# Second half of a weights' product from split factors in three passes

## The chip, the cores and the metric

One core of one Trainium2 chip runs the whole program. The metric is the device time of one execution in microseconds (us). The kernel before took 1076.94, 1076.49 and 1073.06 us in three runs; the median is 1076.49 us.

The engines are named as the profile names them: PE (TensorE, matrix products), PEld (its weight loads), ACT (ScalarE), DVE (VectorE), POOL (GpSimd) and SP (SyncE, which issues most DMAs here). Each works through its own queue strictly in the order in which the program wrote it.

## The reference

An attention over chunks of 32 queries with 56 neighbouring keys and 8 memory keys feeds two gated layers:

```python
attn_out = _attn_ref(**attn_kwargs)             # 4 x 8 heads x 768 x 64
x = attn_out.transpose(0, 2, 1, 3).reshape(B * S, H * D)     # 3072 x 512
# layer 1, d_ff = 1024
a, b = x @ w1, x @ w2
h = a * b @ w3
x = h @ w_out
# layer 2, d_ff = 1536
return ((x @ w_a) * (x @ w_b)) @ w_out2
```

Nothing nonlinear stands between `w3` and `w_out` of layer 1, so the kernel first forms their product W = w3 @ w_out (1024 x 512) and applies it once. The change is in the making of W.

## The kernel before, in words

**Formats.** Most products are made from two parts of each factor: a high part that is the value rounded to the type `float32r`, and a low part that is the value minus the high part. Three matrix passes (high by high, high by low, low by high: `PASSES`) then stand for the float32 product. The product W alone is made in plain `float32`.

**Weights.** The weights arrive as 64-bit words and have to be turned into float32 first. A block goes through a pipeline: `w_load` (DMA, issued on SP, into a raw buffer), `w_scale` (two ACT instructions, lines 372 and 373), `w_sum` (two DVE instructions, lines 377 and 378). Blocks 0 to 7 (`w3a`) hold a row block of `w3` for the first half and the row block of `w_out`; blocks 8 to 11 (`w3b`) hold two row blocks of `w3` each for the second half, so block 8 serves k = 0 and 1 of the second half, block 9 serves k = 2 and 3, and so on; blocks 12 to 27 (`w12`) are the weights w1 and w2, which are split into parts by ACT (line 414) and DVE (line 408). `w_tick` moves every block in the pipeline one step on and issues the next load when a raw buffer is free. In the text, "scale 9" and "sum 9" are these steps of block 9.

**The product W.** Two halves, each 8 steps of k by 4 output tiles m, that is 32 calls of `mm` on 128x128 by 128x512; line 570. Four PSUM banks hold the four tiles; `w_evict` (lines 563 on ACT, 564 on DVE) empties them at the end of a half. After each second call the program drops other work into the engines' queues, by a counter g = 0 to 15: a `w_tick` at listed g, and an `attn_slot`.

**Attention in slots.** Attention goes unit by unit (192 queries, all heads). `attn_slot` takes the next slot of a list made beforehand; slot 0 is at g = 9 of the first half, slot 6 at its g = 15, slots 7 to 22 are g = 0 to 15 of the second half. The stages of a unit: `a_keys` (DVE copy, line 154), `a_scores` (PE, tile sc), `a_max` (DVE, lines 192 and 193), `a_exp` (ACT, line 201, in four parts of 4 exponentials, two parts to a slot), `a_norm` in two parts (DVE lines 216 and 217, then POOL line 218), `a_trans` (PE transposes, tile pt, line 229), `a_pt` (ACT, line 235), `a_pv` (PE, tile xp), `a_x` (ACT line 99, DVE line 102). The slots that matter here: unit 0's scores and all its exponentials in slot 0, its norms in slot 2, its transposes in slot 6 with the scores of unit 1 behind them; unit 1's exponentials in slots 7 and 8, its norms in 8 and 9, its transposes in 12; unit 2's scores in 13, maxima and first exponentials in 14, norms in 15 and 16, transposes in 19, `a_pt` in 20, `a_pv` in 21, `a_x` in 22.

**After W.** The loop over six token blocks follows (`ab_step`: psA and psB, line 619; then psY). The first one needs unit 2's `a_x`. Between its products further `w_tick`s and attention slots are issued. The rest of the program (second layer in a seven-product scheme, lines 812 to 871) follows in the same manner.

**Buffers.** Converted blocks 0 to 11 lie two by two in buffers of the tag "w12" (8 of them in all, which rotate and later hold the split w1 and w2); raw blocks 0 to 11 lie in 4 rotating buffers "raw2".

Of the kernel before, what the change touches and what calls it, by code (L numbers as in the profile page):

```python
# [7 lines left out]
F32 = mybir.dt.float32  # L8
F32R = mybir.dt.float32r
U32 = mybir.dt.uint32  # L10
AF = mybir.ActivationFunctionType
ALU = mybir.AluOpType

P = 128
# [23 lines left out]
CH = 512  # L38
# [7 lines left out]
def tile_attention_moe(  # L46
# [16 lines left out]
    nc = tc.nc  # L63
# [4 lines left out]
    wpool = ctx.enter_context(tc.tile_pool(name="wpool", bufs=8))  # L68
# [4 lines left out]
    p0 = p0stack.enter_context(tc.tile_pool(name="p0", bufs=3))  # L73
# [15 lines left out]
    def mm(o, l, r, first, last):  # L89
        nc.tensor.matmul(o, lhsT=l, rhs=r, start=first, stop=last)  # L90
# [7 lines left out]
    def split_hi(hi, src):  # L98
        nc.scalar.activation(hi, src, AF.Copy)  # L99
# [10 lines left out]
    def a_k(u):  # L110
        if u >= NA:
            return
        k = ks[u] = att.tile([P, NE, 4 * KW], F32, tag="kraw", bufs=1, name="kraw")
        src = kt[2 * NE * u, D : 2 * D].rearrange("d h k -> d (h k)")
        row, x = src.ap
        step = 2 * 2 * D * row[0]
        src = bass.AP(src.tensor, src.offset, [[row[0], P], [step, NE], x])
        nc.sync.dma_start(out=k, in_=src)

    def a_q(u):  # L120
        if u >= NA:
            return
        q = qs[u] = att.tile([P, NE, 4 * GQ], F32, tag="q", bufs=1, name="q")
        src = qt[2 * NE * u : 2 * NE * u + 2 * NE]
        nc.sync.dma_start(
            out=q, in_=src.rearrange("(e r) d h q -> (r d) e (h q)", r=2)
        )
# [18 lines left out]
    def a_keys(u):  # L146
        if u >= NA:
            return
        k = ks.pop(u).rearrange("p e (h k) -> p (e h) k", h=4)
        p, a, e = k.ap  # L150
        win = bass.AP(
            k.tensor, k.offset + NMEM * e[0], [p, a, [CHUNK * e[0], NC], [e[0], KEYS - NMEM]]
        )
        nc.vector.tensor_copy(kw[:, :, :, NMEM:], win)  # L154
        if new_batch(u):
            nc.vector.tensor_copy(
                kw[:, :, :, 0:NMEM], k[:, :, None, 0:NMEM].to_broadcast([P, NH, NC, NMEM])
            )
# [153 lines left out]
    def attn_slot(n=1):  # L312
        for _ in range(n):
            s = acount[0]
            if s >= NEED[-1]:
                return
            acount[0] += 1
            for stage_of, u in todo.get(s, []):
                stage_of(u)
# [18 lines left out]
    def w_tile(i, tag, shape):  # L338
        x = int(tag == "raw2")
        if i < NW0 and tag == "dec":  # L340

            x = int(turn[tag][1] * BUFS[tag][0] < turn[tag][0] * BUFS[tag][1])
        n = BUFS[tag][x]
        if live[tag][x] == n:
            return None, x
        turn[tag][x] += 1
        live[tag][x] += 1
        return (stage, p0)[x].tile(shape, U32, tag=tag, bufs=n, name=tag), x
# [26 lines left out]
    def w_bits(a, r):  # L375
        l, h = r[:, :, 0], r[:, :, 1]
        nc.vector.tensor_scalar(a, h, 3, None, ALU.logical_shift_left)
        nc.vector.tensor_tensor(a, a, l, ALU.add)  # L378
# [5 lines left out]
    def pieces_of(i, *tiles):  # L384
        return [[t[:, c0:c1] for t in tiles] for c0, c1 in pieces(i)]

    def w_sum(i, r):
        kind, f = plan[i][:2]
        if kind == "w12":
            a, ax = w_tile(i, "dec", [P, CH])  # L390
            w_bits(a, r)
            return a.bitcast(F32), ax
        if f % 2 == 0:
            pairs["f"] = wpool.tile([P, 2, 2 * CH], U32, tag="w12", name="w3_f")
        a = pairs["f"][:, f % 2, :]
        for a1, r1 in pieces_of(i, a, r):
            w_bits(a1, r1)
        if kind == "w3a":
            w3k[f], wo_f[f] = a[:, :CH], a[:, CH:]
        else:  # L400
            w3k[8 + 2 * f], w3k[9 + 2 * f] = a[:, :CH], a[:, CH:]
        return None, None

    def w_turn():

        if len(pipe[2]):
            i, a, ax, (d, f, w, hi, lo) = pipe[2].pop(0)
            nc.vector.tensor_tensor(lo, a, hi.bitcast(F32), ALU.subtract)  # L408
            live["dec"][ax] -= 1
            d[f] = w  # L410
        if pipe[1]:
            i, a, ax = pipe[1].pop(0)
            t = w_place(*plan[i][:3])
            nc.scalar.activation(t[3], a, AF.Copy)
            pipe[2].append((i, a, ax, t))
        if len(pipe[0]):
            i, r, tag = pipe[0].pop(0)
            a, ax = w_sum(i, r)
            live[tag][int(tag == "raw2")] -= 1
            if ax is not None:  # L420
                pipe[1].append((i, a, ax))

    def w_next():
        if wraw:
            i, r, tag = wraw.pop(0)
            for (r1,) in pieces_of(i, r):
                w_scale(r1)
            pipe[0].append((i, r, tag))
        while w_load():
            pass  # L430

    def w_tick():
        w_turn()
        w_next()
# [3 lines left out]
    wsm, w3k, wo_f, w12s = {}, {}, {}, {}  # L438
    pairs = {}
# [4 lines left out]
    def w_place(kind, m, c):  # L444

        if c == 0:
            pairs[kind] = wpool.tile([P, 2, 2 * CH], F32R, tag="w12", name="w12")
        w = pairs[kind][:, :, CH * c : CH * (c + 1)]
        v = pairs[kind].rearrange("p l (k j f) -> p l k j f", k=KD, j=2)
        return (w12s if c else {}), m, v, w[:, 0, :], w[:, 1, :]  # L450
# [92 lines left out]
    PASSES = ((0, 0), (0, 1), (1, 0))  # L543
# [17 lines left out]
    def w_evict(half, m):  # L561
        w = wsm[4 * half + m] = w_new(wpool, "wo")
        nc.scalar.activation(w[:, 0, :], banks[m], AF.Copy)
        nc.vector.tensor_tensor(w[:, 1, :], banks[m], w[:, 0, :].bitcast(F32), ALU.subtract)

    for half in range(2):
        banks = [psd.tile([P, 512], F32, tag="d", name="wps") for _ in range(4)]
        for k in range(8):
            for m in range(4):
                mm(  # L570
                    banks[m],
                    w3k[8 * half + k].bitcast(F32)[:, P * m : P * m + P],
                    wo_f[k].bitcast(F32),
                    k == 0,
                    k == 7,
                )
                if k == 7 and m > 0:
                    w_evict(half, m - 1)
                if m % 2 == 0:
                    continue  # L580
                g = 2 * k + m // 2
                if half == 0:
                    if g >= 9:
                        attn_slot()
                    if g in (0, 2, 4, 6, 8, 9):
                        w_tick()
                    if g == 0:
                        a_k(0)
                        a_q(0)
                    if g == 7:  # L590
                        a_keys(0)
                        a_k(1)
                    if g == 9:
                        bound[0] = len(wsrc)
                    if g == 13:
                        w_turn()
                else:
                    attn_slot()
                    if g == 0:
                        w_next()  # L600
                    if g in (1, 4, 5, 6, 9, 10, 11, 12):
                        w_tick()
        w_evict(half, 3)
    del pairs["f"]
    wo_f.clear()
    w3k.clear()
    p0stack.close()

# [421 lines left out]
```

## Time and profile before

| | before |
|---|---|
| median of three runs | 1076.49 us (1073.06 to 1076.94) |
| profiled execution: span from its first to its last instruction | 1073.7 us |
| PE busy | 1058.5 us, 99% |
| ACT busy | 444.0 us, 41% |
| DVE busy | 452.7 us, 42% |
| POOL busy | 233.1 us, 22% |
| PE busy with the product W (tile wps) | 59.2 us |

The profile has one time for the profiled execution, its span; no time around it is recorded, so the span is taken as that execution's own time. It lies 2.8 us under the median and 0.6 us above the lowest of the three runs. Shares are averages over the whole span. In the first 130 us weights arrive, W is made and attention runs between, and DVE and ACT are far busier there than these averages; from about 127 us on PE works without a gap.

A plain float32 call of `mm` shows as two matmul records, a pass on `float32r` operands as one.

### The profile page before, as it was taken

The page shows a single profiled execution, that of the slowest core. Times are in us where ns is not written, and L with a number is a line of the kernel's source. Part 1 is how long each engine was busy: PE and PEld are TensorE (multiplying, and loading weights), DVE is VectorE, ACT ScalarE, POOL GpSimd, SP SyncE. Part 2 cuts the span into 40 slices and gives each one's busy share as a digit, 9 for nine tenths or more (in the row PEclk, how much of TensorE's full clock was granted, in tenths as well). Part 3 has the DMA queues.
Part 4 walks back from the last instruction along what each step waited for, and adds up shares of the span by engine and source line. Part 5 has one row for each costly group of instructions (what it writes and reads, how often), then busy time and mean ns, then how long its engine had stood idle before and what let it go on. Part 6 is the DMA issues. An engine that isn't in the chain of part 4 may idle for free.

```text
span 1073.7 us, 18442 instructions
## 1 busy us (share of the span) xinstructions
PE 1058.5 (99%) x7442; PEld 846.3 (79%) x7442; DVE 452.7 (42%) x751; ACT 444.0 (41%) x1153; POOL 233.1 (22%) x228
## 2 busy tenths in 40 slices
PE   9989899999999999999999999999999999999998
PEld 3457788888888888888888888888888888888886
DVE  5567734435435434346653434432322253223310
ACT  6867654436636543535443343332222232222210
POOL 0102312202303302212033222112233202222210
PEclk9999999999999999999999999999999999999999
DMA  9964474454454462364555554524344433433311
GB/s 365 312 194 158 124 198 146 130 166 146 150 184 118 140 188 86 108 230 143 196 198 206 204 185 157 186 92 154 137 151 173 160 113 139 172 139 138 137 40 39
DMA packets 62342, 172.02 MB, mean 160 GB/s; under 512 B 6321, under 2 KB 21553, under 8 KB 56369
## 3 DMA queue, kind: packets, MB, share of 16 engines
q1 hardware_dynamic: 51680, 104.75, 30.2%
q0 software_dynamic: 10368, 66.06, 17.0%
q8 instruction: 58, 0.95, 0.4%
q14 instruction: 28, 0.22, 0.1%
q10 hardware_dynamic: 208, 0.04, 0.0%
HBM read 137.27 MB, written 33.55 MB: 159 GB/s over the span
## 4 chain that ended last, share of the span: by engine, by line
PE 87%; DVE 1%; ACT 0%; issue 0%; ACTq 0%
PE ps L816 31%; PE ops L90 18%; PE psY L90 12%; PE psB L90 11%; PE psA L90 11%; PE xp L90 2%; PE sc L90 1%; PE pt L229 1%; DVE x L102 0%; DVE tmp L670 0%; ACT x L99 0%; DVE kw L154 0%; DVE w L408 0%; DVE tmp L833 0%; ACT tmp L892 0%
## 5 line engine op out<-in xcount | busy, mean ns | idle before, releaser
L816 PE MATMUL ps<-x,w 128*128 128x512 f32 x1512 | 348.7, 389 | 0.3 <-ACT tmp L828 0.3
L816 PEld LDWEIGHTS ps<-x,w 128*128 128x128 f32 x1512 | 283.6, 188 | 60.1 <-ACT tmp L828 1.4
L833 DVE TENSOR_TENSOR tmp<-ps,tmp 128x512 f32<-128x512 f32 x108 | 74.6, 690 | 261.1 <-PE ps L816 231.0
L90 PE MATMUL psA<-xt,w 128*128 128x512 f32 x576 | 141.7, 394 | 3.0 <-DVE w L408 3.0
L90 PE MATMUL psB<-xt,w 128*128 128x512 f32 x576 | 140.0, 392 | 0.0
L90 PE MATMUL psY<-g,wo 128*128 128x512 f32 x576 | 135.7, 392 | 0.0
L635 POOL TENSOR_TENSOR g<-gv,g 128x512 fp32r<-128x512 f32 x48 | 65.1, 1356 | 305.4 <-ACT g L634 305.4
L828 ACT ACTIVATE tmp<-ps 128x512 f32<-128x512 f32 x108 | 64.6, 599 | 157.8 <-PE ps L816 151.3
L90 PEld LDWEIGHTS psA<-xt,w 128*128 128x128 f32 x576 | 107.3, 188 | 27.9 <-DVE w L408 3.8
L90 PEld LDWEIGHTS psB<-xt,w 128*128 128x128 f32 x576 | 107.2, 188 | 22.5
L90 PEld LDWEIGHTS psY<-g,wo 128*128 128x128 f32 x576 | 107.0, 188 | 22.4
L700 POOL DMA_DIRECT2D w<-wc x72 | 39.7, 553 | 373.6 <-PE ps L816 373.5
L90 PE MATMUL ops<-wo,g 128*128 128x512 f32 x504 | 118.6, 389 | 0.0
L90 PEld LDWEIGHTS ops<-wo,g 128*128 128x128 f32 x504 | 94.6, 188 | 19.6
L839 ACT ACTIVATE g<-tmp 128x512 fp32r<-128x512 f32 x66 | 40.7, 633 | 139.8 <-DVE tmp L838 139.8
L840 POOL TENSOR_TENSOR g<-tmp,g 128x512 fp32r<-128x512 f32 x66 | 84.1, 1294 | 20.4 <-ACT g L839 19.4
L201 ACT ACTIVATE t<-sc,mx 96x64 f32<-96x64 f32 x256 | 75.5, 317 | 25.3 <-DVE mx L193 25.2
L90 PE MATMUL ops<-fo,g 128*128 128x512 f32 x288 | 68.2, 389 | 0.0
L90 PEld LDWEIGHTS ops<-fo,g 128*128 128x128 f32 x288 | 54.1, 188 | 11.2
L90 PE MATMUL wps<-w_f 128*128 128x512 f32 x128 | 59.2, 614 | 0.5 <-DVE w_f L378 0.4
L218 POOL TENSOR_TENSOR t<-t,sm 96x512 f32<-96x512 f32 x32 | 36.8, 1150 | 101.9 <-DVE sm L217 95.4
L372 ACT ACTIVATE raw<-raw 128x512 f32<-128x512 f32 (+1 forms) x66 | 49.3, 748 | 11.4 <-DMA raw<-in_w3a 8.0
(65 smaller groups left out, 878.1 us busy)
## 6 DMA issues: line engine op xcount, KB each, us to landing
w<-wc POOLq DMA_DIRECT2D x36, 1024.0 KB, 6.9
w<-wc POOLq DMA_DIRECT2D x36, 768.0 KB, 5.0
wc<-co SPq DMA_DIRECT2D x84, 256.0 KB
raw<-in_wab SPq DMA_DIRECT2D x24, 512.0 KB
v<-in_vw SPq DMA_DIRECT2D x64, 168.0 KB
kraw<-in_kt SPq DMA_DIRECT2D x16, 512.0 KB
raw<-in_w SPq DMA_DIRECT2D x16, 512.0 KB
raw<-in_w3a SPq DMA_DIRECT2D x6, 1024.0 KB
```

The costliest lines, as they stand in the source:

```text
L90: nc.tensor.matmul(o, lhsT=l, rhs=r, start=first, stop=last)
L201: nc.scalar.activation(t[:, a, r, :], sc[:, r, a, :], AF.Exp, bias=mx[:, r, a : a + 1], scale=SCALE, accum_out=sm[:, a, r : r + 1],)
L218: nc.gpsimd.tensor_tensor(t, t, sm[:, :, :, None].to_broadcast([GQ, 4, 2, KEYS]), ALU.mult)
L229: nc.tensor.transpose(pt[:, a // 4, a % 4, :], t[:, a].rearrange("p r k -> p (r k)"), id_sb)
L372: nc.scalar.activation(h, h, AF.Prelu, scale=2.0**-112, alpha=2.0**32)
L635: nc.gpsimd.tensor_tensor(g2[:, 1, :], gv, g2[:, 0, :].bitcast(F32), ALU.subtract)
L700: nc.gpsimd.dma_start(out=t[:, c0:c1].bitcast(F32), in_=src[:, c0:c1])
L816: nc.tensor.matmul(ps, lhsT=w[:, i, a, k, :], rhs=xs[i][:, b, k, :], start=first and n == 0, stop=n == 5, skip_group_check=not first,)
L828: nc.scalar.activation(z, ps, AF.Copy)
L833: nc.vector.tensor_tensor(z, ps, y, ALU.add)
L839: nc.scalar.activation(g2[:, 0, :], z, AF.Copy)
L840: nc.gpsimd.tensor_tensor(g2[:, 1, :], z, g2[:, 0, :].bitcast(F32), ALU.subtract)
```

## The change

The second half's 32 calls become 32 times three passes on split parts. The split parts of `w3` (name w3h, hi and lo in one tile) are made from each of blocks 8 to 11 by `w_cut`: one ACT copy and one POOL subtraction of 128x1024 each, into the rotating raw2 buffers. It is called at g = 9 to 15 of the first half and, ahead of the attention slot, at every g of the second; it does nothing as long as no summed block waits. The parts of `w_out` (wo_h) are made in the first half, after each k, by `wo_cut`: one ACT copy and one POOL subtraction of 128x512, into buffers of the tag w12. Loads, scales, sums, evictions and the first half's matmuls are as before.

```diff
         if kind == "w3a":
             w3k[f], wo_f[f] = a[:, :CH], a[:, CH:]
         else:
-            w3k[8 + 2 * f], w3k[9 + 2 * f] = a[:, :CH], a[:, CH:]
+            cut.append((f, a.bitcast(F32)))
         return None, None
+
+    w3h, woh, cut = {}, {}, []
+
+    def w_cut():
+        if cut:
+            f, a = cut.pop(0)
+            x = p0.tile([P, 2, 2 * CH], F32R, tag="raw2", bufs=4, name="w3h")
+            split_hi(x[:, 0], a)
+            nc.gpsimd.tensor_tensor(x[:, 1], a, x[:, 0].bitcast(F32), ALU.subtract)
+            for k in range(2):
+                w3h[2 * f + k] = x[:, :, CH * k : CH * k + CH]
+
+    def wo_cut(k):
+        if k % 2 == 0:
+            pairs["h"] = wpool.tile([P, 2, 2, CH], F32R, tag="w12", name="wo_h")
+        x = pairs["h"][:, k % 2]
+        a = wo_f[k].bitcast(F32)
+        split_hi(x[:, 0], a)
+        nc.gpsimd.tensor_tensor(x[:, 1], a, x[:, 0].bitcast(F32), ALU.subtract)
+        woh[k] = x
...
+                if half == 0:
+                    mm(
+                        banks[m],
+                        w3k[k].bitcast(F32)[:, P * m : P * m + P],
+                        wo_f[k].bitcast(F32),
+                        k == 0,
+                        k == 7,
+                    )
+                else:
+                    for i, (a, b) in enumerate(PASSES):
+                        mm(
+                            banks[m],
+                            w3h[k][:, a, P * m : P * m + P],
+                            woh[k][:, b],
+                            k == 0 and i == 0,
+                            k == 7 and i == 2,
+                        )
...
                     if g == 13:
                         w_turn()
+                    if g >= 9:
+                        w_cut()
+                    if m == 3:
+                        wo_cut(k)
                 else:
+                    w_cut()
                     attn_slot()
```

In the queues this stands as follows. In the first half `wo_cut(4)` is written at g = 9, behind unit 0's 16 exponentials and scale 8 on ACT, and ahead of unit 0's norms (g = 11) on POOL. At g = 13 come sum 8, `w_cut` of block 8 and `wo_cut(6)`; at g = 15 `wo_cut(7)`. In the second half `w_cut` of block 9 stands at g = 2 (sum 9 is at g = 1), of block 10 at g = 5 and of block 11 at g = 6.

## Rows read from the trace of the kernel before

**Rows 1.** The page: the chain that ended last, share of the span by engine.

```profile
PE 87%; DVE 1%; ACT 0%; issue 0%; ACTq 0%
```

**Rows 2.** The chain in order of time, its start and a later stretch: start, length, what.

```profile
125.29 0.77 DVE kw L154
...
126.71 1.21 PE psA L90 x4
...
165.52 2.72 PE psA L90 x12
```

**Rows 3.** By stretch: busy us of PE, PEld, DVE, ACT, POOL; clock, DMA share.

```profile
74.00:77.00 3.00, 0.32 (x13) 0.18 (x14) 1.58 (x3) 2.16 (x4) 0.00 (x0) 1.00 0.82 225
77.00:84.00 7.00, 6.96 (x102) 4.14 (x99) 3.22 (x6) 3.03 (x7) 0.00 (x0) 0.52 0.79 236
```

**Rows 4.** Timeline of PE: start, length, line, operation; idle before and its releaser.

```profile
27.27 10.57 PE L90 MATMUL wps<-w_f 128*128 128x512 f32 x24
37.68 0.82 PE L229 MATMUL pt<-id_sb,t 96*128 96x96 f32 x8
40.59 1.18 PE L90 MATMUL sc<-kw,q 64*32 64x64 f32 x96 [2.08 <-DMA q<-in_qt]
41.70 5.42 PE L90 MATMUL wps<-w_f 128*128 128x512 f32 x12
47.05 1.60 PE L90 MATMUL xp<-p,v 64*64 64x32 f32 x96
...
56.59 1.19 PE L90 MATMUL sc<-kw,q 64*32 64x64 f32 x96
...
70.51 3.62 PE L90 MATMUL wps<-w_f 128*128 128x512 f32 x8
76.82 2.50 PE L90 MATMUL xp<-p,v 64*64 64x32 f32 x96 [2.69 <-ACT p L235]
79.25 3.78 PE L90 MATMUL wps<-w_f 128*128 128x512 f32 x4
82.50 4.04 PE L90 MATMUL psA<-xt,w 128*128 128x512 f32 x12
```

**Rows 5.** Timeline of ACT, the product W's stretch.

```profile
27.41 1.14 ACT L372 ACTIVATE raw<-raw 128x1024 f32<-128x1024 f32 x1 [2.64 <-DMA raw<-in_w3a]
...
34.11 1.17 ACT L372 ACTIVATE raw<-raw 128x1024 f32<-128x1024 f32 x1
...
36.17 2.31 ACT L563 ACTIVATE wo<-wps 128x512 fp32r<-128x512 f32 x4
...
43.33 0.31 ACT L201 ACTIVATE t<-sc,mx 96x64 f32<-96x64 f32 x1 [3.98 <-DVE mx L193]
...
52.08 0.84 ACT L99 ACTIVATE xt<-xp 128x768 fp32r<-128x768 f32 x1
...
61.13 0.31 ACT L201 ACTIVATE t<-sc,mx 96x64 f32<-96x64 f32 x1 [3.09 <-DVE mx L193]
```

**Rows 6.** Timeline of DVE, the same stretch.

```profile
34.91 1.69 DVE L154 COPY kw<-kraw 128x1344 f32<-128x1344 f32 x1 [0.22 <-DMA kraw<-in_kt]
...
37.34 1.23 DVE L378 CUSTOM_DVE_ANT_0 w_f<-raw,w_f 128x2048 uint16<-128x2048 uint16 x1
...
48.11 1.22 DVE L378 CUSTOM_DVE_ANT_0 w_f<-raw,w_f 128x2048 uint16<-128x2048 uint16 x1
...
53.83 0.85 DVE L154 COPY kw<-kraw 128x1344 f32<-128x1344 f32 x1
...
66.69 1.42 DVE L378 CUSTOM_DVE_ANT_0 dec<-raw,dec 128x1024 uint16<-128x1024 uint16 x1
```

**Rows 7.** Timeline of POOL, the same stretch.

```profile
34.84 1.04 POOL L218 TENSOR_TENSOR t<-t,sm 96x512 f32<-96x512 f32 x1 [1.30 <-DVE sm L217]
...
66.51 1.05 POOL L218 TENSOR_TENSOR t<-t,sm 96x512 f32<-96x512 f32 x1 [1.20 <-DVE sm L217]
```

**Rows 8.** POOL subtractions of one tile: min/median/max ns, first and last start.

```profile
L635 POOL TENSOR_TENSOR g<-gv,g x48: 1279/1295/1786, 94.2 to 508.9; 128x512 fp32r<-128x512 f32 x48
```

More of the change, by code (lines that the diff above doesn't have):

```diff
@@ L569, in tile_attention_moe @@
             for m in range(4):
[L570 to L576, printed above, removed]
+                if half == 0:
[15 more added lines that the diff above has]
+                        )
                 if k == 7 and m > 0:
@@ L603, in tile_attention_moe @@
         w_evict(half, 3)
-    del pairs["f"]
+    del pairs["f"], pairs["h"]
     wo_f.clear()
+    woh.clear()
+    w3h.clear()
     w3k.clear()
```

## The prediction

> **What bounds the kernel now.** I read the chain of waits first: 87% of the span is PE [rows 1], and traced back from the end the chain is PE with hardly a break until 126.7 us, where it leaves PE for DVE (key copy, then w1/w2) [rows 2]. From there on nothing in this change matters; what counts is when PE gets to 126.7. The stretches tell where PE is not the bound before that: it is busy 0.32 of 3 us in 74 to 77 and then works 7 us at a granted clock of 0.52, that is 1.2 GHz nearly throughout [rows 3]. PE's own timeline gives the half in question: the second half begins at 41.70, scores of unit 2 stand at 56.59, PE then waits 2.69 us at 76.82 for ACT's `a_pt` of unit 2, and psA begins at 82.50 [rows 4]. That wait is the end of a chain of maxima, exponentials, norms, sums 13 and 14, loads and scales, not of matmuls: PE was through with its calls at 74.1 (70.51 + 3.62). So the second half is set by the attention's chain on ACT and DVE, with PE 2.7 us ahead of it.
>
> **The change: matmuls.** 24 records in 10.57 us, the last 0.59 long, are 0.434 us apart, so a float32 call of two records costs 0.868 [rows 4]. A split pass costs 2.72/12 = 0.227 in a full train [rows 2], a call of three 0.68. PE's work falls by 32 x 0.188 = 6.0 us. This is a gain only where PE is the bound.
>
> The Trainium skill, "FP8 and Floating Point Precision" (TensorE Precision Notes), says that true float32 takes four passes. By it a pass is 0.868/4 = 0.217 and the cut 32 x 0.217 = 6.9 us; the row of this kernel's own split train is taken.
>
> **First half, until g = 9.** Each `wo_cut` adds 0.58 us on ACT (four evictions take 2.31) [rows 5] and 1.29 on POOL [rows 8], the median. ACT waits 2.64 us for block 7's data at 27.41 [rows 5], which absorbs cuts 0 to 3 (2.3 us), and POOL is empty there. Nothing is added to any DMA queue, and raw loads shift by tenths while the data are late anyway: cost nothing; if that cover were gone, 2.3 us.
>
> **End of the first half.** `wo_cut(4)` stands on ACT behind the exponentials and scale 8, so its copy begins at 36.17, where the evictions began [rows 5]. Its POOL part stands ahead of unit 0's two norms, which now wait for it; the first half's transposes wait for the norms. DVE's key copy at 34.91 took 1.69 instead of 0.85 while POOL's norm ran [rows 6, 7]; with the norm gone from there sum 8 is done at 38.57 - 0.84 = 37.75. The POOL part is written to begin at 36.8, but DVE's sum runs then. L378 took 1.42 us for 1024 elements beside the POOL instruction of 66.51, and 1.23 for 2048 alone [rows 6, 7]: one waits for the other, and the later one loses. So it runs 37.75 to 39.05, the norms (1.04 each [rows 7]) to 41.15, transposes from 41.2, not 37.68. Transposes 0.66 and scores 1.11 [rows 4] give a second half that starts at 43.0: **+1.3**. (The scores could not start before 40.59, when q lands, in either case.) The evictions on ACT, behind the cut of block 8 and those of `w_out`, end at 42.3 and their DVE parts before 43.0: hidden; unit 1's exponentials start at 43.33 + 1.3 = 44.65.
>
> **Price of a `w_cut`.** ACT: two instructions of 128x1024 take 36.17 - 34.11 = 2.06 [rows 5], 1.03 each. POOL has no row of 1024 elements; the nearest is 1.29 for 512 [rows 8]. It costs at least 1.29, and at most 3.6, twice the longest of the 512 rows with DVE in the way (1.79). I take twice 1.29, 2.6, since it is the same instruction with twice the elements.
>
> **Second half.** POOL goes on after the norms with `wo_cut(5)` (to 42.45) and block 8 (to 45.05). The first call's third pass needs the low part of block 8: PE waits from 43.45 to 45.05, finishes k = 0 at 47.3, two calls, unit 0's `a_pv` (1.6 [rows 4], 0.07 of it overlapping) and two more calls at 51.6. Then k = 2 needs block 9. Its ACT copy is behind unit 1's exponentials and scales 9 and 10: 52.08 - 43.33 = 8.75 after the first of them [rows 5], so 53.4 to 54.45; the POOL part ends at 57.05. Before, k = 2 needed only sum 9, which ended at 49.3 [rows 6]. **PE now stands 5.4 us at k = 2.** Behind that POOL part is unit 1's second norm, and behind the waiting matmul all of PE: rest of k = 2, transposes, two calls, then unit 2's scores at 61.3 instead of 56.59 [rows 4].
>
> Unit 2's exponentials, 61.13 before [rows 5], are now the latest of three:
> - PE: scores end at 62.4, and from scores to exponentials it is 43.33 - 41.77 = 1.56: 64.0 at full clock. After 2.69 us of standing the clock was 0.52 for 7 us [rows 3]; this stand is longer, so I expect it again. Passes at half rate for the first 4 to 7 us after it add 2 to 3 us: up to 67.
> - ACT: its own work from 43.33 to 58.04 is 14.7 us (3.09 idle follow); three cuts add 3.1: 62.45. The copy of block 10 also waits for sum 10, which stands on DVE behind `a_x` and the key copy, blocked by block 9's POOL part until 57.05: sum 10 at 60.0, where ACT could have gone on at 57.2: 65.2.
> - DVE: sum 12 stands ahead of unit 2's maxima and meets POOL's parts of blocks 10 and 11 (61.1 to 66.3). If it gets in between them, exponentials start at 66.4, if behind both, 68.6.
>
> I take 67.5, **+6.4**. From there to `a_pv` of unit 2 (15.7 us) the chain is unchanged, so PE comes to 83.2 there and still stands some 4 us before it, as its remaining calls are shorter. After it the two last calls took 3.25 us at the low clock (79.25 to 82.50); six passes at the same ratio take 2.6: **-0.6**. In the first token block ACT and DVE pass the delay on: exponentials of unit 3 wait for scores behind psA. Sum: **+5.8 us**, span 1079.5, and on the median of the runs, 2.8 above this execution's span, 1082.3.
>
> On the lock between DVE and POOL the Trainium skill, "SBUF — State Buffer" (Who interferes with whom), says that the shared port pair is exclusive for a whole instruction and that a DVE instruction with two SBUF inputs meets a POOL instruction that reads SBUF; the loser waits to its end. The trace agrees (1.42 for half of the elements that take 1.23 alone). By the rule the evictions, with PSUM as one input, stay free; without any lock the DVE limit would be about 64 and ACT's 65 would decide, a sum of +3.4.
>
> **Buffers.** The new tiles rotate over tiles whose last readers (matmuls and POOL parts at least two k earlier) are done: no wait. The first `av` over the freed raw2 space is written after psA: nothing. A missed reader would cost up to a k, 2.7 us.
>
> **The rivals.**
> - *PE is the bound* (not slower): if the low parts come before PE needs them, the second half shrinks by 6.0: 1070.5. For it: PE's rows from 41.70 to 70.51 show no wait [rows 4]. It decides at one place, whether block 9's POOL part ends before PE reaches k = 2 (about 51). Against it: sum 9 alone ended at 49.3, and copy and subtraction take 3.6 more with empty queues. 4%.
> - *Stand and saving cancel*: the late k = 2 costs PE 5.4, its shorter calls return it, and exponentials slip only by ACT's queue (+1.3 and the three copies less the idle 3.09): +0.7 or so, 1077. 11%.
> - *Late chain, no lock, no low clock*: +2 to +4.7, centre +3.4, 1079.9. 27%.
> - *Forecast*: +4.7 to +8.5, 1082.3. 50%.
> - *All of it worse*: PE's idle time 37.84 to 41.2 also brings the low clock (+1.4), and the POOL parts of blocks 9 to 11 cost 3.6 (+1 each): +8.5 to +13, 1087. 8%.
>
> **How the numbers follow.** A difference under 0.5%, 5.4 us, can hardly be told from none. Faster by that much is the first rival: 0.04. Slower: the part of the forecast above +5.4 (a little more than four fifths, 42%) and the last rival: 0.50. Within: 0.46. The range 1076.5 to 1088 leaves out the first rival and the ends of the second and last; the forecast's own is 1081.2 to 1085.
>
> **What would show it.** In the trace after: PE waiting for POOL about 1.5 us near 43.5 and 5 us near 52 to 57; POOL parts of 2.6 us; norms of unit 0 after 39 us; scores of unit 2 past 61 and psA near 88; lengthened L377/L378 beside POOL; the low clock after 57 and again at the end of the half. It is wrong if PE passes k = 2 without a wait for POOL, or if psA begins before 82.5.

## The result, and the profile after

The changed kernel takes 1084.13 us (median of four runs, 1083.33 to 1086.98), the kernel before 1076.72 in the same comparison (four runs): a ratio of 1.0083, interval 1.0063 to 1.0104. It is slower by 7.4 us, more than the 5.4 that count as a difference; the forecast was +5.8. The profiled execution after is the slowest of its four (1086.98 us, span 1085.1; the other spans are 1081.6 to 1082.9), so its rows show a loss of 11.4 us in the span, 4.0 more than the medians have. In every execution with both figures the time is 1.7 to 1.9 us longer than the span, so the traced execution before (span 1073.7) took some 1075.5 us, 1.0 under its median and not the 2.8 that the span alone suggests. That is about 1 of the 4.0; the rest is the execution after, which lies 2.9 above its median. Its mean granted clock is 0.988, that of the other three 0.993; over the span that is, by estimate, some 11 us more at the lower level of 1.2 GHz. This could account for the 2.3 to 3.7 us by which the others are faster, but without their traces the stretch is not known.

PE's timeline after, to be laid beside [rows 4] (start, length, what; in brackets the idle time before and what ended it):

```profile
27.35 1.19 PE L90 MATMUL sc<-kw,q 64*32 64x64 f32 x96 [0.92 <-DVE kw L156]
...
41.52 1.90 PE L229 MATMUL pt<-id_sb,t 96*128 96x96 f32 x8 [2.48 <-POOL t L218]
43.36 1.94 PE L90 MATMUL sc<-kw,q 64*32 64x64 f32 x96
45.23 5.80 PE L90 MATMUL wps<-wo_h,w3h 128*128 128x512 f32 x18
...
57.20 0.74 PE L90 MATMUL wps<-wo_h,w3h 128*128 128x512 f32 x2 [3.04 <-ACT w3h L99]
59.68 4.63 PE L90 MATMUL wps<-wo_h,w3h 128*128 128x512 f32 x10 [1.75 <-POOL w3h L411]
...
66.92 1.19 PE L90 MATMUL sc<-kw,q 64*32 64x64 f32 x96
68.05 4.38 PE L90 MATMUL wps<-wo_h,w3h 128*128 128x512 f32 x18
...
87.50 2.79 PE L90 MATMUL xp<-p,v 64*64 64x32 f32 x96 [3.78 <-ACT p L235]
90.22 2.80 PE L90 MATMUL wps<-wo_h,w3h 128*128 128x512 f32 x6
93.04 0.50 PE L90 MATMUL psA<-xt,w 128*128 128x512 f32 x1
...
137.02 2.03 PE L90 MATMUL psA<-xt,w 128*128 128x512 f32 x4 [2.23 <-DVE w L428]
```

The stand at k = 2 is there: 3.04 us for block 9's ACT copy, then, after the two passes that need only block 9's high part, 1.75 for its low part from POOL. Unit 2's scores, at 56.59 before, start at 66.92, and psA at 93.04 instead of 82.50. From there nothing is given back: the last wait of the first token block ends at 137.02 instead of 126.71 [rows 2]. Behind this wait the clock falls once more (granted clock 0.50 from 137.1 to 140.5), which it did not do behind the same wait (2.21 us) of the kernel before, and psY starts at 151.63 instead of 139.75: of these 11.9 us, 10.5 are there at psA and 1.3 come after it. POOL after (L421 are the parts of `w_out`, L411 those of blocks 8 to 11):

```profile
38.67 1.80 POOL L421 TENSOR_TENSOR wo_h<-w_f,wo_h 128x512 fp32r<-128x512 f32 x1 [11.49 <-ACT wo_h L99]
40.44 2.03 POOL L218 TENSOR_TENSOR t<-t,sm 96x512 f32<-96x512 f32 x2
...
43.67 2.35 POOL L411 TENSOR_TENSOR w3h<-w_f,w3h 128x1024 fp32r<-128x1024 f32 x1
...
57.22 2.41 POOL L411 TENSOR_TENSOR w3h<-w_f,w3h 128x1024 fp32r<-128x1024 f32 x1 [5.77 <-ACT w3h L99]
...
64.30 5.53 POOL L411 TENSOR_TENSOR w3h<-w_f,w3h 128x1024 fp32r<-128x1024 f32 x2 [3.06 <-ACT w3h L99]
```

DVE after, early in the first half and then sum 12 (the first two dec rows) with unit 2's maxima behind it:

```profile
23.20 2.09 DVE L378 CUSTOM_DVE_ANT_0 w_f<-raw,w_f 128x2048 uint16<-128x2048 uint16 x1
...
25.98 1.31 DVE L156 COPY kw<-kraw 128x192 f32<-128x192 f32 x1
...
64.93 2.63 DVE L377 TENSOR_SCALAR dec<-raw 128x512 uint32<-128x512 uint32 x1
67.70 2.68 DVE L378 CUSTOM_DVE_ANT_0 dec<-raw,dec 128x1024 uint16<-128x1024 uint16 x1
70.30 1.21 DVE L192 TENSOR_REDUCE mx<-sc 96x16 f32<-96x1024 f32 x1
```

L377 and L378 of sum 12 need 0.4 and 0.7 us when POOL is idle (the run that moves them, below, has the rows). Here they end at 67.57 and 70.38, some 0.3 and 0.5 us behind the two POOL parts of 64.30, which end at 67.28 and 69.83. Granted clock by stretch after, columns as in [rows 3]:

```profile
42.00:52.00 10.00, 9.90 (x193) 7.68 (x191) 5.41 (x9) 6.85 (x24) 7.53 (x6) 0.68 0.93 316
52.00:57.00 5.00, 2.15 (x46) 1.50 (x38) 1.59 (x3) 5.00 (x19) 0.00 (x0) 1.00 0.85 223
57.00:64.00 7.00, 5.06 (x12) 3.66 (x13) 5.96 (x6) 3.72 (x5) 4.02 (x2) 0.61 0.27 87
88.00:92.00 4.00, 4.00 (x92) 3.65 (x89) 1.26 (x2) 0.52 (x2) 0.00 (x0) 0.50 0.86 267
```

Three stands of PE (2.48 us for POOL, 4.8 in two pieces at k = 2, 3.78 for `a_pt`) and the last wait of 2.23 are each followed by a stretch in which much or all of the time has the lower level of 1.2 GHz.

### The profile page after: what moved, and what is told of

Same layout as the page of the kernel before. It is cut to its first block, busy times and chain, and to the rows that moved or that the text cites. A ratio compares the mean times of both kernels' runs of the same rounds, so it can differ in the third digit from the quotient of the medians.

```text
span 1085.1 us, 18529 instructions
## 1 busy us (share of the span) xinstructions
PE 1061.3 (98%) x7474; PEld 857.9 (79%) x7474; DVE 461.3 (43%) x751; ACT 451.5 (42%) x1165; POOL 256.4 (24%) x240
## 4 chain that ended last, share of the span: by engine, by line
PE 86%; DVE 1%; ACT 0%; issue 0%; ACTq 0%
PE ps L853 31%; PE ops L90 18%; PE psY L90 12%; PE psB L90 11%; PE psA L90 11%; PE xp L90 2%; PE sc L90 1%; PE pt L229 1%; DVE x L102 0%; DVE tmp L707 0%; ACT x L99 0%; DVE kw L154 0%; DVE w L428 0%; DVE tmp L870 0%; ACT tmp L929 0%
## 5 line engine op out<-in xcount | busy, mean ns | idle before, releaser
L671 ACT ACTIVATE g<-gv 128x512 fp32r<-128x512 f32 x48 | 30.5, 634 | 57.7 <-DVE gv L670 57.6
L201 ACT ACTIVATION_READ_ACCUMULATOR t<-sc,mx 96x1 f32 x256 | 54.1, 211 | 0.0
```

The costliest lines, as they stand in the source:

```text
L201: nc.scalar.activation(t[:, a, r, :], sc[:, r, a, :], AF.Exp, bias=mx[:, r, a : a + 1], scale=SCALE, accum_out=sm[:, a, r : r + 1],)
L671: nc.scalar.activation(g2[:, 0, :], gv, AF.Copy)
```

## The experiments

All are the changed or the old kernel with small edits. The places at which each run's trace was read, in us: first exponentials of units 1 and 2 (ACT), scores and `a_pv` of unit 2 and the first psA (PE); "chain" is from unit 2's first exponentials to psA; ratio to the kernel before with its interval.

| | exp 1 | scores 2 | exp 2 | a_pv 2 | psA | chain | ratio |
|---|---|---|---|---|---|---|---|
| before | 43.33 | 56.59 | 61.13 | 76.82 | 82.50 | 21.37 | |
| after | 47.38 | 66.92 | 71.81 | 87.50 | 93.04 | 21.23 | 1.0083 |
| passes only | 43.22 | 56.13 | 60.99 | 76.58 | 82.03 | 21.04 | 1.0000 (0.9987 to 1.0013) |
| cuts only | 47.21 | 65.11 | 71.65 | 87.37 | 92.42 | 20.77 | 1.0104 (1.0081 to 1.0127) |
| no POOL parts | 44.30 | 61.42 | 64.20 | 80.82 | 86.36 | 22.16 | 1.0039 (1.0023 to 1.0054) |
| norms first | 46.91 | 66.56 | 71.36 | 87.01 | 92.55 | 21.19 | 1.0094 (1.0066 to 1.0122) |
| block parts on DVE | 49.70 | 66.46 | 74.01 | 89.64 | 93.31 | 19.30 | 1.0095 (1.0074 to 1.0116) |
| sum 12 later | 47.35 | 65.65 | 69.71 | 85.30 | 89.78 | 20.07 | 1.0073 (1.0050 to 1.0096) |
| before, steps moved | 42.00 | 55.23 | 59.78 | 72.71 | 76.64 | 16.86 | 0.9959 (0.9943 to 0.9975) |
| split, rearranged | 46.21 | 58.96 | 61.74 | 76.41 | 80.36 | 18.62 | 1.0013 (1.0001 to 1.0025) |
| steps moved, passes only | 44.45 | 57.36 | 62.23 | 75.66 | 79.33 | 17.10 | 0.9959 (0.9944 to 0.9974) |
| after, steps moved | 47.30 | 66.05 | 71.75 | 85.14 | 88.82 | 17.07 | 1.0057 (1.0041 to 1.0073) |

**Passes only.** No `w_cut`, no `wo_cut`; the second half multiplies one pair of tiles, copied once.

```diff
-                            w3h[k][:, a, P * m : P * m + P],
-                            woh[k][:, b],
+                            one[:, P * m : P * m + P],
+                            one[:, CH:],
...
-                    w_cut()
                     attn_slot()
...
```

> The kernel after without any of the cuts: the second half runs its three passes on one pair of tiles that two ACT copies make at the start of the first half (so the second half's product is of block 0 with itself, not of w3 and w_out). This is the saving of 6.0 us on PE alone, with nothing to wait for. My theory (the second half is set by the chain of unit 2's maxima and exponentials on DVE and ACT): psA begins at 81 to 82.5 us, unit 2's exponentials at 60 to 61.2, PE stands 6 to 8 us before unit 2's a_pv, and the time is 0 to 1.5 us under the kernel before. Rival (PE bounds the second half): psA at 76.5, the time 6 us under the kernel before.

Measured 1075.69 us beside 1075.49. PE's two costliest waits up to 100 us (releaser, total, times, longest):

```profile
PE pt L229 <- DVE xt L102: 3.9, 2, 2.1
PE xp L90 <- ACT p L235: 2.1, 1, 2.1
```

The shorter calls turn into 3.9 us of waiting for the transposes; unit 2's exponentials come at 60.99 instead of 61.13. The stand before unit 2's `a_pv` is 2.1 us and not the 6 to 8 expected: the rest of the saving went into these waits and into slower passes behind the second of them (12 passes at 69.90 took 4.58 us, about 3.0 at full clock). The saving on PE by itself is worth nothing here that the interval (1.4 us either way) would show.

**Cuts only.** The cuts stay, the calls are float32 again.

```diff
-                if half == 0:
+                if True:
                     mm(
                         banks[m],
-                        w3k[k].bitcast(F32)[:, P * m : P * m + P],
+                        w3k[8 * half + k].bitcast(F32)[:, P * m : P * m + P],
...
```

> The kernel after with all its cuts on ACT and POOL, but the second half's matmuls in plain float32 as before, so no matmul reads a cut. My theory (the cuts delay the attention's chain: norms behind a POOL part, sum 12 and the maxima behind POOL parts): unit 2's exponentials start at 70 to 72 us as in the kernel after (71.8), psA at 92 to 94, and the time is 7 to 9 us over the kernel before. Rival (the loss is PE's wait for the cuts at k = 2 and the low clock behind it): without that wait psA at 83 to 86 and 0.5 to 3 us over the kernel before.

Measured 1086.58 us. No product waits for a cut in this kernel, and yet unit 2's exponentials come at 71.65, within 0.2 us of the changed kernel's. So the stand at k = 2 is not needed for the loss: what the cuts do to ACT, DVE and POOL is enough for all of it. The time is 11.1 us over the kernel before, above the 7 to 9 expected and above the changed kernel's 7.4. The intervals of the two ratios overlap, so whether the shorter calls give something back once the cuts are there is not shown.

**No POOL parts.** The ACT copies stay; the subtractions go, and the passes use high parts alone.

```diff
-            nc.gpsimd.tensor_tensor(x[:, 1], a, x[:, 0].bitcast(F32), ALU.subtract)
...
-        nc.gpsimd.tensor_tensor(x[:, 1], a, x[:, 0].bitcast(F32), ALU.subtract)
...
```

> The kernel after without the POOL subtractions: ACT's copies stay, and the three passes all read high parts (the low parts' share of the product is left out). My theory (POOL's parts are the larger cost, through its queue and the lock with DVE): unit 0's transposes at 37.5 to 39.5, PE waits 2 to 4 us at k = 2 for ACT's copy of block 9, unit 2's exponentials at 63 to 65, psA at 84 to 87, the time 1.5 to 4 us over the kernel before. Rival (ACT's added copies are the cost): psA stays at 90 or later, 6 us or more over the kernel before.

Measured 1079.5 us; exponentials of unit 2 at 64.20. PE's longest waits:

```profile
PE wps L90 <- ACT w3h L99: 5.6, 1, 5.6
PE xp L90 <- ACT p L235: 4.6, 1, 4.6
```

Of the 10.7 us at unit 2's exponentials the ACT copies make 3.1 and the POOL parts 7.6. The stand at k = 2 is longer than expected, 5.6 us instead of 2 to 4, and for the copy alone; scores and exponentials still come earlier, since unit 1's exponentials start 3.1 us earlier (44.30, not 47.38) and no POOL part follows the copy. In the time the shares are more even: the ratio is 1.0039 with the copies alone and 1.0083 with both, and at psA 3.9 of the 10.5 us are left, as the chain from the exponentials on is longer here (22.16).

**Norms first.** `wo_cut(4)`'s POOL part is put behind unit 0's norms.

```diff
+    late = []
...
-        nc.gpsimd.tensor_tensor(x[:, 1], a, x[:, 0].bitcast(F32), ALU.subtract)
+        late.append((x, a))
+        if k != 4:
+            while late:
+                y, b = late.pop(0)
+                nc.gpsimd.tensor_tensor(y[:, 1], b, y[:, 0].bitcast(F32), ALU.subtract)
```

> The kernel after with one instruction moved: POOL's part of wo_cut(4) is written behind unit 0's two norms instead of ahead of them. My theory: unit 0's transposes go from 41.5 to 39 or earlier, unit 1's scores to about 41, unit 1's exponentials from 47.4 to 45.6 (now behind the evictions), and the whole chain by 1.5 to 2 us: psA at 90.5 to 91.5, the time 5 to 6 us over the kernel before instead of 7.4. Rival (the norms' place does not matter, because k = 2 waits for block 9 in any case): psA stays at 92.5 to 93.5.

A miss: 1086.08 us, exponentials of unit 1 at 46.91 where 45.6 was expected, and psA at 92.55, in the rival's range. PE's timeline there:

```profile
38.57 0.82 PE L229 MATMUL pt<-id_sb,t 96*128 96x96 f32 x8
39.55 1.18 PE L90 MATMUL sc<-kw,q 64*32 64x64 f32 x96 [0.15 <-DMA q<-in_qt]
43.55 4.86 PE L90 MATMUL wps<-wo_h,w3h 128*128 128x512 f32 x12 [2.81 <-DVE wo L589]
```

Transposes and scores came as early as expected. What holds unit 1 then is the other line of work: ACT's copies for block 8 and `w_out` stand ahead of the evictions, DVE's part of the evictions (L589 in this kernel) starts at 42.80, and the maxima, behind it in DVE's queue, at 45.40. The copy of block 8 itself waited for sum 8 until 40.71: with the norms out of the way, sum 8's L378 met a POOL part of `w_out` and took 2.29 us, where it took 1.23 in the changed kernel. The prediction had costed exactly these evictions as hidden.

**Block parts on DVE.** The four subtractions of 128x1024 go from POOL to DVE.

```diff
-            nc.gpsimd.tensor_tensor(x[:, 1], a, x[:, 0].bitcast(F32), ALU.subtract)
+            nc.vector.tensor_tensor(x[:, 1], a, x[:, 0].bitcast(F32), ALU.subtract)
```

> The kernel after with the subtractions of blocks 8 to 11 on DVE instead of POOL; those of w_out stay on POOL. My theory (7.6 us of the 10.7 by which unit 2's exponentials are late come from POOL's parts, most of it sum 12 on DVE blocked by POOL's parts of blocks 10 and 11): each subtraction takes 1.2 to 1.4 us, sum 12's two instructions return to 0.43 and 0.69, unit 2's exponentials start at 65 to 67.5 us, psA at 87 to 89.5, the time 3 to 5 us over the kernel before. Rival (the work counts, not the lock: DVE gets 5 us more in front of the maxima): exponentials at 70 or later, 7 us or more over.

A miss as well, in the rival's range: 1086.36 us, exponentials of unit 2 at 74.01. DVE at the end of the first half, and POOL beside it:

```profile
40.33 5.55 DVE L411 TENSOR_TENSOR w3h<-w_f,w3h 128x1024 fp32r<-128x1024 f32 x1 [1.12 <-ACT w3h L99]
45.80 2.47 DVE L584 TENSOR_TENSOR wo<-wps,wo 128x512 fp32r<-128x512 f32 x4
48.19 1.21 DVE L192 TENSOR_REDUCE mx<-sc 96x16 f32<-96x1024 f32 x1
```

```profile
40.29 2.04 POOL L218 TENSOR_TENSOR t<-t,sm 96x512 f32<-96x512 f32 x2
42.29 4.71 POOL L421 TENSOR_TENSOR wo_h<-w_f,wo_h 128x512 fp32r<-128x512 f32 x3
```

Block 8's subtraction took 5.55 us; later ones, with POOL idle, 1.23. It began beside the norms and ended while POOL was still at the parts of `w_out`, with evictions and maxima queued behind it. The collision had been moved, not removed. That sets unit 1's exponentials (49.70). At unit 2 it is the rival, DVE's added work: sum 12 takes 0.42 and 0.69 us again and the scores come at 66.46, but the maxima start only at 72.48, behind sum 12 and block 11's subtraction, which had waited for its ACT copy until 70.27.

**Sum 12 later.** Block 12's step goes behind unit 2's maxima.

```diff
+                    if g == 6:
+                        w_next()
+                    if g == 7:
+                        w_turn()
+                        while w_load():
+                            pass
-                    if g in (1, 4, 5, 6, 9, 10, 11, 12):
+                    if g in (1, 4, 5, 9, 10, 11, 12):
```

> The kernel after with sum 12 written behind unit 2's maxima instead of ahead of them; nothing else changes its length. My theory: the maxima start as soon as the scores are in PSUM (68.1) since they read PSUM and are not blocked by POOL, unit 2's exponentials at 69.3 to 69.8 instead of 71.8, psA 1 to 2.3 us earlier (90.7 to 92), the time 5 to 6.5 us over the kernel before. Rival (the maxima are blocked by POOL's parts as well): exponentials at 71 or later.

Unit 2's maxima on DVE, with sum 12 behind:

```profile
66.88 1.22 DVE L192 TENSOR_REDUCE mx<-sc 96x16 f32<-96x1024 f32 x1 [1.90 <-PE sc L90]
68.14 1.48 DVE L193 TENSOR_SCALAR mx<-mx 96x16 f32<-96x16 f32 x1
69.53 0.41 DVE L377 TENSOR_SCALAR dec<-raw 128x512 uint32<-128x512 uint32 x1
70.08 0.69 DVE L378 CUSTOM_DVE_ANT_0 dec<-raw,dec 128x1024 uint16<-128x1024 uint16 x1
```

The exponentials come at 69.71, in the range expected (69.3 to 69.8), and sum 12 takes 0.41 and 0.69. But that place is hit by luck: the maxima could start 1.2 us earlier than expected (66.88, not 68.1), and L193, 0.17 us with POOL idle, took 1.48 beside POOL's part, which ran to 69.58. The reduction L192 beside the same parts kept its 1.22. So sum 12 behind two POOL parts is worth 2.1 us at this place, and the next limit is a POOL part again, now through L193. The time, 1084.02, is 7.8 over and not 5 to 6.5; it cannot be told from the changed kernel's.

**Before, steps moved.** In the kernel before, the two block steps of g = 11 and 12 go to 13 and 14, past unit 2's `a_pt`.

```diff
-                    if g in (1, 4, 5, 6, 9, 10, 11, 12):
+                    if g in (1, 4, 5, 6, 9, 10, 13, 14):
```

> The kernel before with two ticks (those of g = 11 and 12 of the second half) moved to g = 13 and 14, behind unit 2's a_pt on ACT. If the second half's end is set by ACT's queue (a_pt behind scale 17 and its load), a_pt starts at 70.7 instead of 75.97, PE does not stand before unit 2's a_pv, the clock does not fall at 77, psA begins at 77.5 to 79, and the time is 3.5 to 5 us under the kernel before. Rival (the w1/w2 blocks are then late for the first token block and PE waits there instead): psA early, but PE continuous from 126 as before, no change in the time.

Measured 1071.58 us beside 1076.19: faster than both kernels, as expected. The reason is in ACT's queue. In the kernel before a scale that waits for its transfer stands ahead of `a_pt` (L235); the changed kernel has the same order, with a wait of 1.19 us at 85.53:

```profile
74.84 0.68 ACT L372 ACTIVATE raw<-raw 128x512 f32<-128x512 f32 x1 [1.15 <-DMA raw<-in_w]
75.42 0.66 ACT L373 ACTIVATE raw<-raw 128x512 uint32<-128x512 uint32 x1
75.97 0.80 ACT L235 ACTIVATE p<-pt 128x768 f32<-128x768 f32 x1
```

With the steps moved, `a_pt` starts at 69.35 instead of 75.97, PE no longer stands before `a_pv`, the low clock behind that stand goes too, and the chain from exponentials to psA is 16.86 us instead of 21.37. These 4.5 us are the edit's; psA itself is 5.9 us earlier, but 1.3 of that is there before the edit can act, since unit 1's scores did not wait for q in this execution (39.25 instead of 40.59).

**Split, rearranged.** The change with all subtractions on DVE, cuts earlier, blocks 9 to 11 and the later steps rescheduled (core of the edit):

```diff
-            nc.gpsimd.tensor_tensor(x[:, 1], a, x[:, 0].bitcast(F32), ALU.subtract)
+            split_lo(x[:, 1], a, x[:, 0])
...
+                    attn_slot()
+                    if g in (0, 2, 7):
+                        w_turn()
+                    if g in (0, 3, 8):
+                        w_cut()
...
-                    if g in (1, 4, 5, 6, 9, 10, 11, 12):
+                    if g in (9, 10, 11, 13):
```

> The three passes kept, the cuts rearranged: all subtractions on DVE, the copies of w_out's parts as soon as their sums are done, scale and sum of block 9 ahead of unit 1's exponentials, of 10 and 11 where ACT and DVE would stand, and ticks 12 and on behind unit 2's exponentials. If the lateness of the cuts is all that ate the 6 us, PE does not stand at k = 2, unit 2's exponentials start at 57.5 to 60, psA at 74 to 78, and the time is 4 to 8 us under the kernel before. Rival (ACT's and DVE's added work is the bound wherever it is put): psA at 80 or later, no gain over the kernel before.

Measured 1077.58 us, ratio 1.0013: no better than the kernel before, though the stand at k = 2 is gone and unit 2's exponentials come at 61.74. Of the 5.7 us between its span and that of the old kernel with its steps moved (1074.7 and 1069.0), 3.7 are lost before psA (80.36 and 76.64). About 3 more go in the first token block, and 1 comes back behind it; PE in that stretch:

```profile
120.55 2.08 PE L90 MATMUL psA<-xt,w 128*128 128x512 f32 x4 [3.33 <-DVE w L428]
...
140.46 7.87 PE L90 MATMUL psY<-g,wo 128*128 128x512 f32 x34
```

From psA to psY it takes 60.1 us, in the old kernel with its steps moved 57.0 (76.64 to 133.66): PE waits 4.3 us in all for split blocks of w1 and w2 there instead of 3.0, and from 120 to 140 the granted clock is 0.91 instead of 1.00. The edit puts the steps of these blocks later, which would explain the longer waits; no run tests it alone, and another order of the steps was not tried. Unit 2's exponentials were expected at 57.5 to 60, psA at 74 to 78 and the time 4 to 8 us under: all missed. The place of psA and the time are the rival's, by which the added work is the bound wherever it is put.

**Steps moved, passes only.** The old kernel with steps moved has no stand on PE over 0.5 us from 40 to 76.64, so the shorter calls had their best chance there. The edits are those of the two runs above.

> The kernel before with two edits: the two block steps moved from g = 11 and 12 to 13 and 14, as in the run that did that alone, and the second half's product from three passes on one pair of tiles copied once (the product of block 0, not the weights' product), so that the 6.0 us on PE are saved and nothing is cut. With float32 in the second half, PE there worked from 40 to 76.64 with no stand over 0.5 us, so this is the place in which the saving could be worth something. Theory (the chain of unit 2 is just behind PE): first exponentials at 59.5 to 60, transposes of unit 2 at about 67.8 instead of 68.49, a_pv(2) at 69.7 to 71 instead of 72.71, first psA at 73.5 to 75 instead of 76.64; the time 1.5 to 3 us under that of the run with the block steps alone, 1068.5 to 1070. Rival A (PE is the bound there): 6 us earlier, 1065.5. Rival B (the chain was the bound there too): nothing, 1071.5.

Measured 1071.37 us, the ratio the same as without the passes, so rival A is out and rival B fits best; a gain of a microsecond or two would hide in the intervals. In its profiled execution unit 1's scores waited 2.45 us for a transfer of q until 40.90 (39.25 in the run with the steps alone) and the passes behind ran at the low clock, so all its places in the table are later; the chain alone is 17.10 us beside 16.86. PE there:

```profile
70.50 1.05 PE L229 MATMUL pt<-id_sb,t 96*128 96x96 f32 x8 [1.79 <-DVE xt L102]
71.25 4.48 PE L90 MATMUL wps<-one 128*128 128x512 f32 x12
```

The saved time becomes a wait of 1.79 us for unit 1's `a_x`, and the 12 passes behind it take 4.48 us where 12 take about 3.0 at full clock.

**After, steps moved.** The same move of steps in the changed kernel.

> The changed kernel with the two block steps of the second half moved from g = 11 and 12 to 13 and 14 and nothing else. Theory: the cuts' cost up to the first exponentials of unit 2 stays (70 to 72), but the four block conversions no longer lie in ACT's queue between these exponentials and the eviction of p, so that a_pv(2) comes 13 to 14 instead of 15.7 us behind them and the first psA at 87 to 90 instead of 93.04: 3 to 6 us faster than the changed kernel, 1078 to 1081, and still slower than the kernel before with the same move (1071.6) by 7 to 10. Rival (the cuts fill ACT and DVE there by themselves): no gain, 1083 to 1085.

psA at 88.82 and the chain at 17.07 us came as expected; the time, 1082.21 us, is above the 1078 to 1081 expected. By the ratios the move is worth 0.0026, 2.8 us (3 to 6 expected), by psA 4.2; the changed kernel's traced execution, its slowest, may be what makes the second number large. Against the old kernel with the same move (1.0057 to 0.9959) the change still costs 10.5 us (7 to 10 expected): the two edits act on different links of one chain, and mending the later link doesn't pay for the earlier one.

## Why the prediction was right, and where its sizes were off

Direction, mechanism and range held. Its reading that the half is set by the attention's chain is shown by the passes alone (worth nothing) and the cuts alone (at least all of the loss). Step by step:

- **Matmuls, 6.0 us less.** Six calls take 4.38 us instead of 5.42 [rows 4], so 0.173 a call and 5.5 in all. Slightly over; it decided nothing.
- **First half until g = 9, "cost nothing".** Wrong. ACT's wait did absorb the copies, but the step looked at ACT and POOL alone. The POOL parts of `w_out` block DVE's sums and key copies (L378 2.09 us, L156 1.31), and unit 0's scores start at 27.35 instead of 26.15: 1.2 us at that place. Without POOL parts they start at 26.23.
- **End of the first half, +1.3.** The transposes were forecast at 41.2, behind both norms. The first four came at 41.52, behind one norm, and the second norm ended at 42.47: POOL's part had begun 0.9 us later than forecast and took 1.80 us, not 1.29. Transposes and scores then ran at the lower clock, which the prediction had there only in the rival "all of it worse"; the second half began at 45.23 instead of 43.0, L193 took 0.64 us beside a POOL part, and unit 1's exponentials came at 47.38, not 44.65. This miss of 2.7 us is the largest up to there. The clause "hidden" on the evictions failed too, as the run with the norms first showed: they are late by the copies ahead of them on ACT. Their DVE parts were not slowed: 0.68 to 0.69 us each beside a busy POOL, as the prediction had it.
- **Price of a `w_cut`.** 2.6 us taken for the POOL part; 2.35, 2.41, 2.98 and 2.58 measured. ACT's copy 1.03, measured 1.04 to 1.09.
- **Stand at k = 2.** Forecast 5.4 us up to 57.05; measured 4.8, up to 59.68. The cause named first, the copy behind unit 1's exponentials in ACT's queue, is the larger part (3.04).
- **Three limits for unit 2's exponentials, 67.5.** They came at 71.81. All starts were 2 to 3 us late by the step above. PE's limit was lengthened by the low clock, as forecast (ten passes 4.63 us): scores at 66.92, forecast 61.3 and with that clock 2 to 3 later. DVE decided: sum 12 met both POOL parts, the far end of the range given.
- **Chain and last two calls.** 15.69 us from the exponentials to `a_pv` both before and after: unchanged, as forecast. The last calls took 2.82 instead of 3.25 at the low clock, but psA followed `a_pv` after 5.54 us instead of 5.68: -0.1, not -0.6, since `a_pv` itself now ran wholly at that clock (2.72 us up to the last calls instead of 2.43).
- **After psA, nothing added.** psY lost 1.3 us more to the low clock behind the last wait of the first token block, a term that the sum does not have.

So the term that was mis-sized is the delay at unit 2's exponentials: +6.4 forecast, +10.7 in the profiled execution. By the medians the total missed by only 1.6 us, which is better than its steps are; as far as the trace goes, the near hit of the total is luck. What stays open: the changed kernel's three faster runs lie 2.3 to 3.7 us under the one that the trace shows, and no row tells which stretch is shorter in them. The cuts alone, at 1086.31 to 1087.18 in four runs, agree with the slowest one.

## What to carry to other kernels

Cutting the matmuls of a stretch pays only if PE is what ends it; here an order of two block steps in ACT's queue was worth 4.6 us and, without cuts, 32 shorter calls nothing measurable. Preparing operands costs time on the engines that feed the chain: an instruction on POOL has to be charged also to DVE instructions that meet it, in stretches where DVE looks free as well. Here these were the sums, the key copies and L193, and a subtraction; those that read PSUM kept their lengths beside POOL (evictions 0.69 us, L192 1.22, L102 0.96). And a stand of PE can cost slower passes behind it wherever it comes, not only where the kernel before showed one. It need not: a stand of 3.28 us before the transposes at 56.76 in the rearranged kernel was followed by a clock of 1.00.

## What the runs showed of the hardware that was not expected

- A DVE subtraction of 128x1024 with both inputs in SBUF took 5.55 us (40.33 to 45.87) beside POOL instructions of 1.04, 1.04, 1.27, 1.27 and 2.25 us, 4.3 more than alone. That is longer than any single one of them, so it was held by more than one in a row. The last of them, nearly 1 us longer than its like, began at 44.75, 1.1 us before the subtraction ended: it looks as if DVE came in there, though no row says so. Sum 12's two instructions each waited for one.
- A DVE instruction as small as L193 (96x16, 0.17 us) took 1.48 us beside a POOL subtraction.
- The Trainium skill, "SBUF — State Buffer" (Who interferes with whom), says that whoever issues first has the shared port pair for its whole instruction and that the other blocks until then. Sum 12 and L193 agree with it, since each of these waits ended within 0.6 us of a POOL part's end. The 5.55 us do not: POOL's instructions ended at 41.33, 42.33 and 43.56, and had DVE come in at any of these it would have been done by 44.8, not at 45.87. There the measurement decides: a DVE instruction can be passed over while POOL works through a queue without a gap.
- While PE was busy 2.15 of 5 us (52 to 57) the granted clock still read 1.00; it was 0.61 in the stretch after.
